# A new order for the instructions of all five engines in a two-layer linear-attention and SwiGLU kernel

## The chip, the cores and the metric

The kernel runs on one core of a Trainium2 chip. The metric is the device time in microseconds (us) of one execution. Five engines work side by side: TensorE (PE in the profile; its weight loads PEld), VectorE (DVE), ScalarE (ACT), GpSimd (POOL) and SyncE (SP), which here only issues DMA transfers.

## What is computed

Two layers on x of 2048 rows and 512 columns, each a linear attention with 32 heads and a gated MLP with 1792 hidden columns, both behind a layer norm and added to x:

```
def _A_ref(x, wqkv, wo):
    qkv = (x @ wqkv).reshape(B, S, 3, H, Dh) ...
    phi = lambda t: jnp.where(t > 0, t + 1, jnp.exp(t)) + 1e-6
    pq, pk = phi(q), phi(k)
    kv = jnp.einsum("bhsd,bhse->bhde", pk, v)
    z = jnp.einsum("bhsd->bhd", pk)
    o = einsum("bhqd,bhde->bhqe", pq, kv) / (einsum("bhqd,bhd->bhq", pq, z)[..., None] + 1e-6)
    return o ... @ wo

def _B_ref(x, w1, w3, w2):
    return (_silu(x @ w1) * (x @ w3)) @ w2

x = x + _A_ref(_layernorm(x), wqkv, wo)
x = x + _B_ref(_layernorm(x), w1, w3, w2)
# and both once more, with the same weights
```

## The kernel before

Each product is made of three matmuls of 16-bit parts: every operand is split into a high and a low part (fp16), and high by high, high by low and low by high are added in PSUM (`mm`, L947). The products of the MLPs and of the second attention are further cut into 2 x 2 blocks, of which seven products instead of eight are made (`products7`).

The work runs in stages. First the keys of layer 0, 16 tiles of 128 rows (`keys_turn`): ScalarE and another engine make high and low parts of a tile, SP issues a DMA transpose (L1858), `keep_transposed` stores an earlier tile's transpose to DRAM (L1875) for use by the queries, and PE makes the keys (`pk`) and the Gram products (`gt`). Then the queries, the MLP of layer 0, and from about 545 us on the second attention (`attention7`). Its keys go in 8 pairs of tiles (`pair_turn`): ScalarE (L1586) and POOL (L1587, L1588, L1589) split the pair's rows, SP issues a transpose of 12 blocks (L1590); ScalarE (L1591) and POOL (L1592) split the sums of rows that the seven products need, and SP issues a transpose of 16 blocks (L1593) and a store of the pair (L1594). PE makes the seven products into the banks kb, ka and kc; ScalarE takes a bank (L1634) or VectorE adds it (L1638), which frees it for the next product. The feature map follows (L1675 to L1681), and PE's Gram products `gt`. The layer norm's scale is POOL's: L917 to L921, with a pow in L918, and ScalarE's L924 applies it.

The queries (about 640 to 735 us) read the pair's transposes back from DRAM (`load7`, L1685), make seven products into qb, qa and qc, and the exp of L1717 and L1718. Then come the weighing (L1732 to L1753), the split (L1759 on ScalarE, L1760 on POOL), a transpose (L1769) and the output product `po`, which VectorE and ScalarE add to x (L1953 to L1958). The MLP of layer 1 starts on the first of these rows, and its last sums are stored to the output (L2127).

What sets the order on every engine is a table: `ORDER` (L72 to L475) holds for each engine a permutation of the instructions in the sequence in which the code issues them, and `arrange` makes each instruction depend on the one ahead of it in the table, with no wait between engines:

```
for engine, text in ORDER.items():
    at = []
    for part in text.split():
        first, _, last_ = part.partition("-")
        at.extend(range(int(first), int(last_ or first) + 1))
    for before, after in zip(at, at[1:]):
        tc.add_manual_dep(traced[engine][after], traced[engine][before].name, ...NoSync...)
```

An engine runs its list in that order and stops at the first instruction whose inputs or buffers are not ready, whatever stands behind it. SP's list is the order in which the transfers are issued.

Of the kernel before, what the change touches and what calls it, by code (L numbers as in the profile page):

```python
# [73 lines left out]
        "0-20 22-23 26-27 24 28 25 30 29 34 38-39 35-36 21 31-32 37 40-41 33 42-65 78-89 66-77 "  # L74
        "102-113 90-92 96-101 93-95 126-137 120-122 114-116 123-125 117-119 150-161 144-149 "
        "162-173 138-140 174-176 183-185 141-143 180-182 177-179 186-197 201-203 198-200 204-209 "
        "228-230 225-227 210-224 231-245 258-269 255-257 249-254 246-248 276-278 282-293 279-281 "
        "306 300-302 307 303-305 308-319 270-272 326-328 273-275 294-299 323-325 350-352 347-349 "
        "329-331 353-355 332-343 320-322 377-379 344-346 356-367 380-391 404 371-373 405-406 "
        "374-376 398-400 368-370 401-403 395-397 392-394 416-418 407-409 413-415 419-421 410-412 "  # L80
        "425-427 431 422-424 428-430 432-455 460-471 456-458 472-483 459 484-555 568-579 556-567 "
        "592-603 616-627 580-591 604-615 628-651 664-675 652-663 688-699 676-687 712-723 700-711 "
        "736-747 760-771 724-735 748-759 772-808 821-832 809-820 833-868 893-904 869-880 905-910 "
        "917-928 881-892 911-916 941-958 965-970 929-934 1001-1006 935-940 971-976 959-964 "
        "1007-1012 977-988 1109 1013-1018 1049-1054 1110-1111 1085-1090 1019-1024 1112 1117-1120 "
        "1055-1060 989-994 1121 1113 1122 1114 995-1000 1115-1116 1373-1374 1125 1381 1126 1375 "
# [82 lines left out]
        "3780-3781 3784-3785 3815-3816 3788-3789 3722-3727 3786-3787 3728-3733 3764-3769 "  # L169
        "3752-3757 3819-3820 3734-3745 3821-3822 3831 3823-3828 3857-3862 3791-3796 3803-3808 "  # L170
        "3817-3818 3833 3797-3802 3809-3814 3829 3835 3832 3848-3849 3834 3830 3836-3837 "
        "3863-3868 3838-3839 3844-3847 3840-3841 3856 3850 3842-3843 3854 3852 3855 3853 3851 "
        "3869-3874 3917-3918 3893-3898 3875-3880 3921-3924 3899-3904 3881-3886 3905-3910 "
        "3887-3892 3911-3916 3925-3926 3962-3967 3933 3919-3920 3931 3927-3928 3935 3929-3930 "
        "3968-3973 3998-4002 3937 3934 3950-3961 4034-4035 3938-3943 4042 4026-4029 4003 "
        "3944-3949 3932 3974-3979 4038-4039 4022-4023 3936 4024-4025 3980-3985 4030-4031 "
        "4067-4070 4036-4037 4081 4032-4033 4004-4009 3986-3991 4010-4015 4040-4041 4082 "
        "4088-4089 3992-3997 4071-4076 4083 4079-4080 4016-4021 4077-4078 4109-4114 4090-4091 "
        "4087 4084 4145-4150 4102 4092-4093 4115-4120 4055-4060 4151-4156 4061-4066 4094-4095 "
        "4100-4101 4121-4126 4085 4108 4104-4105 4157-4162 4103 4127-4132 4043-4048 4086 "  # L180
        "4169-4170 4163-4168 4133-4138 4096-4097 4139-4144 4049-4054 4098-4099 4106 4214-4219 "
        "4173-4174 4220-4225 4250-4255 4171-4172 4107 4190-4195 4202-4213 4175-4176 4185 4183 "
        "4177-4178 4181-4182 4189 4184 4274-4275 4286-4287 4226-4231 4196-4201 4179-4180 "
        "4256-4261 4232-4237 4276-4277 4262-4267 4186 4278-4279 4288 4280-4281 4187 4290 4294 "
        "4289 4291 4188 4238-4249 4268-4273 4319-4320 4282-4285 4323-4324 4321-4322 4292 "
        "4333-4334 4340-4341 4293 4325-4326 4307-4312 4327-4328 4335-4336 4313-4318 4295-4300 "
        "4331-4332 4342-4343 4354 4301-4306 4382-4387 4329-4330 4355 4388-4393 4412-4417 "
        "4337-4338 4348-4349 4339 4352-4353 4350-4351 4344-4345 4358 4360 4359 4394-4405 "
        "4346-4347 4356-4357 4406-4411 4361-4362 4365-4366 4487-4492 4363-4364 4481-4486 "
        "4367-4368 4375 4369-4370 4377 4373-4374 4376 4371-4372 4418-4421 4432-4433 4381 "  # L190
        "4379-4380 4426-4427 4430-4431 4438 4378 4428-4429 4422-4425 4434 4436 4435 4439-4440 "
        "4437 4499-4504 4493-4498 4441-4446 4517-4522 4455-4456 4464-4465 4447-4448 4511-4516 "
        "4453 4466-4467 4454 4476 4449-4450 4460-4461 4457-4458 4468-4469 4477 4470-4471 "
        "4462-4463 4478-4479 4451-4452 4474 4459 4472-4473 4480 4475 4535-4540 4505-4510 "
        "4523-4525 4553-4558 4526-4534 4544-4549 4541-4543 4565-4570 4559-4564 4550-4552 "
        "4577-4588 4601-4606 4571-4576 4595-4597 4592-4594 4610-4612 4598-4600 4589-4591 "
        "4613-4615 4607-4609 4619-4624 4616-4618 4631-4636 4625-4630 4649-4654 4643-4648 "
        "4661-4663 4637-4642 4667-4672 4664-4666 4655-4657 4679-4681 4658-4660 4685-4690 "
        "4682-4684 4673-4678 4697-4702 4691-4696 4715-4720 4709-4714 4703-4708 4733-4738 "
        "4724-4729 4742-4744 4730-4732 4721-4723 4745-4747 4751-4756 4739-4741 4748-4750 "  # L200
        "4763-4768 4757-4762 4781-4786 4775-4780 4769-4774 4799-4804 4790-4798 4787-4789 "
        "4814-4816 4811-4813 4805-4810 4817-4828 4847-4852 4859-4861 4829-4834 4856 4835-4846 "
        "4862-4864 4877-4879 4865-4870 4857-4858 4880-4882 4874-4876 4883-4888 4853-4855 "
        "4871-4873 4895-4900 4889-4894 4913-4918 4907-4912 4973-4978 4901-4906 4931-4936 "
        "4928-4930 4922-4924 4979-4990 5003-5008 4946-4948 4919-4921 4991-4996 4940-4942 "
        "4937-4939 4997-5002 4949-4951 4961-4963 5009-5014 4925-4927 5015 4952-4954 5016-5021 "
        "4964-4966 4943-4945 5028-5033 4958-4960 5110-5115 5040-5045 5022-5027 4955-4957 "
        "4967-4972 5052-5057 5122-5127 5034-5039 5116-5121 5046-5051 5058-5069 5134-5139 "
        "5070-5106 5128-5133 5107-5109 5146-5151 5140-5145 5152-5169 5206-5212 5170-5181 "
        "5213-5217 5182-5199 5230-5241 5200-5205 5218-5229 5260-5265 5296-5301 5242-5247 "  # L210
        "5272-5283 5254-5259 5284-5295 5266-5271 5248-5253 5302-5307 5326-5331 5308-5313 "
# [2246 lines left out]
```

## Time and profile before

| | |
|---|---|
| median of 3 runs | 1137.07 us (1136.81 to 1137.78) |
| span of the profiled execution | 1134.0 us |
| PE busy | 1123.7 us, 99% |
| DVE busy | 849.3 us, 75% |
| ACT busy | 663.2 us, 58% |
| POOL busy | 429.7 us, 38% |

The profile is one execution. PE's matmuls are pipelined, and the stated end of one lies behind the start of the next; a stall is therefore read as the distance of two starts less the spacing of the matmuls between them. The idle time in brackets behind a row is what the profile counts between the stated end and the next start, with the engine or transfer that ended it.

### The profile page before, as it was taken

The page shows a single profiled execution, that of the slowest core. Times are in us where ns is not written, and L with a number is a line of the kernel's source. Part 1 is how long each engine was busy: PE and PEld are TensorE (multiplying, and loading weights), DVE is VectorE, ACT ScalarE, POOL GpSimd, SP SyncE. Part 2 cuts the span into 40 slices and gives each one's busy share as a digit, 9 for nine tenths or more (in the row PEclk, how much of TensorE's full clock was granted, in tenths as well). Part 3 has the DMA queues.
Part 4 walks back from the last instruction along what each step waited for, and adds up shares of the span by engine and source line. Part 5 has one row for each costly group of instructions (what it writes and reads, how often), then busy time and mean ns, then how long its engine had stood idle before and what let it go on. Part 6 is the DMA issues. An engine that isn't in the chain of part 4 may idle for free.

```text
span 1134.0 us, 22473 instructions
## 1 busy us (share of the span) xinstructions
PE 1123.7 (99%) x9117; PEld 888.3 (78%) x9117; DVE 849.3 (75%) x1468; ACT 663.2 (58%) x1104; POOL 429.7 (38%) x477
## 2 busy tenths in 40 slices
PE   8999999999999999999999999999999999999998
PEld 3445446888888888888886676578888888888887
DVE  7789878896978887889896488847855666465556
ACT  7668878775544445455578666686544434343442
POOL 6731796502001222335678416862152110302113
PEclk9999999999999999999999999999999999999999
DMA  8995665389673332331267946643482440220001
GB/s 258 304 292 181 174 136 121 75 220 272 204 279 122 117 149 103 112 155 66 48 179 177 276 165 153 114 89 105 120 240 102 177 178 1 85 84 29 11 20 57
DMA packets 171768, 162.94 MB, mean 144 GB/s; under 512 B 139536, under 2 KB 147984, under 8 KB 167056
## 3 DMA queue, kind: packets, MB, share of 16 engines
q1 hardware_dynamic: 171664, 161.51, 48.7%
q8 instruction: 71, 1.16, 0.4%
q14 instruction: 33, 0.27, 0.1%
HBM read 80.08 MB, written 47.32 MB: 112 GB/s over the span
## 4 chain that ended last, share of the span: by engine, by line
PE 91%; DVE 2%; POOL 2%; DMA 2%; issue 1%; ACT 1%; SPq 0%; DVEq 0%; POOLq 0%; ACTq 0%
PE bb L947 26%; PE po L2097 20%; PE bc L947 13%; PE ba L947 6%; PE gt L947 6%; PE po L947 5%; PE pq L947 4%; PE pk L947 3%; PE po L2117 3%; DMA arena<-arena 2%; PE kb L947 1%; PE qb L947 1%; PE kc L947 1%; PE kv L947 0%; PE qc L947 0%
## 5 line engine op out<-in xcount | busy, mean ns | idle before, releaser
L947 PEld LDWEIGHTS <-arena 128*128 128x128 f16 x6648 | 646.1, 98 | 204.5 <-DMA arena<-arena 4.4
L947 PE MATMUL bb<-arena 128*128 128x256 f16 x2688 | 349.2, 273 | 0.0
L2097 PE MATMUL po<-arena 128*128 128x256 f16 x2058 | 288.5, 273 | 0.0
L2052 ACT ACTIVATE arena<-bb 128x512 f32<-128x512 f32 x196 | 115.3, 594 | 195.5 <-PE bb L947 166.7
L2097 PEld LDWEIGHTS <-arena 128*128 128x128 f16 x2058 | 201.3, 98 | 23.4
L947 PE MATMUL bc<-arena 128*128 128x256 f16 x1344 | 179.6, 273 | 0.0
L2055 DVE TENSOR_TENSOR arena<-arena,bc 128x512 f32<-128x512 f32 x112 | 76.7, 685 | 87.5 <-PE bc L947 54.1
L2007 ACT ACTIVATE arena<-arena,scalars 128x512 f32<-128x512 f32 x112 | 74.6, 666 | 90.2 <-DVE arena L2055 70.2
L2146 DVE SCALAR_TENSOR_TENSOR arena<-po,scalars,arena 128x256 f32<-128x256 f32 (+1 forms) x180 | 101.5, 585 | 31.7 <-PE po L2097 21.7
L2013 DVE TENSOR_TENSOR arena<-arena 128x1280 f16<-128x1280 f32 (+1 forms) x90 | 105.4, 1174 | 21.2 <-ACT arena L2011 20.8
L2011 ACT ACTIVATE arena<-arena 128x512 f16<-128x512 f32 (+1 forms) x112 | 101.0, 904 | 32.2 <-DVE arena L2026 13.7
L2008 DVE SCALAR_TENSOR_TENSOR arena<-arena,scalars 128x512 f32<-128x512 f32 x112 | 78.6, 705 | 34.5 <-ACT arena L2007 34.4
L947 PE MATMUL ba<-arena 128*128 128x256 f16 x672 | 91.8, 273 | 0.0
L947 PE MATMUL gt<-arena 128*128 128x512 f16 x384 | 89.6, 379 | 0.0
L947 PE MATMUL po<-arena 128*128 128x512 f16 x384 | 86.8, 379 | 0.5 <-DMA arena<-arena 0.5
L2013 POOL TENSOR_TENSOR arena<-arena 128x512 f16<-128x512 f32 x22 | 27.0, 1228 | 115.0 <-ACT arena L2011 108.2
L2155 POOL TENSOR_TENSOR arena<-arena 128x512 f32<-128x512 f32 x27 | 38.0, 1406 | 81.7 <-DVE arena L2146 81.7
L2154 POOL TENSOR_TENSOR arena<-arena 128x512 f32<-128x512 f32 x27 | 37.1, 1375 | 71.4 <-DVE arena L2146 69.3
L871 DVE SCALAR_TENSOR_TENSOR arena<-arena,scalars 128x512 f16<-128x512 f32 (+2 forms) x74 | 59.1, 814 | 2.3 <-ACT arena L869 2.2
L924 ACT ACTIVATE arena<-arena,nb_all,rs_all 128x512 f32<-128x512 f32 x64 | 50.8, 806 | 13.2 <-POOL nb_all L921 7.6
L2023 POOL TENSOR_TENSOR arena<-arena 128x256 f32<-128x256 f32 x10 | 7.9, 786 | 131.3 <-DVE arena L2008 131.3
L869 ACT ACTIVATE arena<-arena,scalars 128x512 f16<-128x512 f32 (+2 forms) x74 | 52.2, 718 | 5.2 <-DVE arena L1003 2.3
(234 smaller groups left out, 1449.4 us busy)
## 6 DMA issues: line engine op xcount, KB each, us to landing
arena<-xb_d SPq DMA_DIRECT2D x12, 1792.0 KB, 8.0
xb_d<-arena SPq DMA_DIRECT2D x8, 1792.0 KB, 7.7
w_d<-arena SPq DMA_DIRECT2D x5, 1792.0 KB, 7.6
arena<-w_d SPq DMA_DIRECT2D x5, 1792.0 KB, 8.0
arena<-in_B_w_dram SPq DMA_DIRECT2D x8, 896.0 KB, 7.0
arena<-in_B_w_dram SPq DMA_DIRECT2D x28, 256.0 KB, 3.0
xt_d<-arena SPq DMA_DIRECT2D x8, 896.0 KB, 5.1
arena<-xt_d SPq DMA_DIRECT2D x8, 896.0 KB, 6.7
```

What stands on the lines that cost most here:

```text
L869: nc.scalar.activation(hi, src, AF.Copy, scale=scale)
L871: lambda: nc.vector.scalar_tensor_tensor(lo, src, scale, hi, OP.mult, OP.subtract)
L924: nc.scalar.activation(dst, x_sb[:, t, :], AF.Identity, scale=rs_all[:, t : t + 1], bias=nb_all[:, t : t + 1],)
L947: nc.tensor.matmul(dst, lhs(a, k), rhs(b, k), start=first and k == 0 and i == 0, stop=last and k == n - 1 and i == len(PASSES) - 1, skip_g ...
L2007: nc.scalar.activation(t, gate, AF.Silu, scale=info["u1"])
L2008: nc.vector.scalar_tensor_tensor(t, up, info["hid"], t, OP.mult, OP.mult)
L2011: nc.scalar.activation(hs[:, 0, lo:hi], t[:, lo:hi], AF.Copy)
L2013: engine.tensor_tensor(hs[:, 1, lo:hi], t[:, lo:hi], hs[:, 0, lo:hi], OP.subtract)
L2052: nc.scalar.activation(dst, bank_, AF.Copy)
L2055: nc.vector.tensor_tensor(dst, dst, bank_, OP.add)
L2097: nc.tensor.matmul(po[:, i * HALF : (i + 1) * HALF], hs[:, a, qx, cs], w2[:, b, qw, :], start=g == ends[0] and i + a + b == 0, stop=g == e ...
L2146: nc.vector.scalar_tensor_tensor(dst, src, cb, to, OP.mult, OP.add)
```

## The change

Only the table `ORDER` is new. Each engine's list is another permutation of the same instructions: on PE 864 of 9100 stand at another place, on VectorE 439 of 1436, on ScalarE 272 of 1051, on POOL 176 of 475, on SP 120 of 307, by at most 25 places and on average by about one. The table is 8 lines longer, so the same line of code has a number that is higher by 8 in the changed kernel. The lists differ from before in the first keys (20 to 195 us), from about 500 to 735 us, in single places up to 935 us, and in the last 40 us. There are four loads of ScalarE's function tables in both. Two lines of the diff show its kind:

```diff
-        "102-113 90-92 96-101 93-95 126-137 120-122 114-116 123-125 117-119 150-161 144-149 "
...
+        "66-77 102-113 90-92 99-101 93-98 126-137 117-119 123-125 114-116 150-161 120-122 "
```

On SP, at the tiles 2 to 4 of the first keys, before (L962 loads a weight, L2319 a tile of x, L1875 stores a tile's transpose, L1858 is the transpose):

```order
L1875 DMA xt_d<-arena 128x1024
L1858 DMA_TRANSPOSE arena<-arena 128x8x128
L962 DMA arena<-in_B_w_dram 128x1792
L1875 DMA xt_d<-arena 128x1024
L1858 DMA_TRANSPOSE arena<-arena 128x8x128
L2319 DMA arena<-in_A_x_dram 128x512 x2
L1875 DMA xt_d<-arena 128x1024
```

and after:

```order
L1883 DMA xt_d<-arena 128x1024
L2327 DMA arena<-in_A_x_dram 128x512 x2
L1866 DMA_TRANSPOSE arena<-arena 128x8x128
L970 DMA arena<-in_B_w_dram 128x1792
L1883 DMA xt_d<-arena 128x1024 x2
L1866 DMA_TRANSPOSE arena<-arena 128x8x128
```

Two loads of x have moved ahead of tile 3's transpose (the first one here), and the store of tile 3, which stood behind tile 4's transpose, stands ahead of it, beside the store of tile 2.

On SP again, in the keys of the second attention from pair 3 to pair 5, before (L1590 and L1593 are a pair's transposes, L1594 its store):

```order
L1590 DMA_TRANSPOSE arena<-arena 128x12x128
L1593 DMA_TRANSPOSE arena<-arena 128x16x128
L1590 DMA_TRANSPOSE arena<-arena 128x12x128
L1593 DMA_TRANSPOSE arena<-arena 128x16x128
L1594 DMA xt_d<-arena 128x3584 x2
L1590 DMA_TRANSPOSE arena<-arena 128x12x128
L1593 DMA_TRANSPOSE arena<-arena 128x16x128
L1594 DMA xt_d<-arena 128x3584
```

and after:

```order
L1598 DMA_TRANSPOSE arena<-arena 128x12x128
L1601 DMA_TRANSPOSE arena<-arena 128x16x128
L1602 DMA xt_d<-arena 128x3584
L1598 DMA_TRANSPOSE arena<-arena 128x12x128
L1601 DMA_TRANSPOSE arena<-arena 128x16x128
L1602 DMA xt_d<-arena 128x3584
L1598 DMA_TRANSPOSE arena<-arena 128x12x128
L1601 DMA_TRANSPOSE arena<-arena 128x16x128
```

The store of pair 3 has moved from behind the transposes of pair 4 to the place ahead of them.

On POOL, between the L1592 of pair 5 and that of pair 6, before:

```order
L1592 TENSOR_TENSOR arena<-arena 128x1024
L1654 COPY arena<-scalars 128x2
L917 TENSOR_SCALAR ve<-mv_all 128x2
L920 TENSOR_SCALAR neg<-mv_all 128x2
L1588 TENSOR_TENSOR arena<-arena 128x512
L918 TENSOR_TENSOR rs_all<-ve,minus_half 128x2
L1587 CAST arena<-arena 128x2x256
L1589 TENSOR_TENSOR arena<-arena 128x2x256
L921 TENSOR_TENSOR nb_all<-neg,rs_all 128x2
L1592 TENSOR_TENSOR arena<-arena 128x1024
```

and after:

```order
L1600 TENSOR_TENSOR arena<-arena 128x1024
L1662 COPY arena<-scalars 128x2
L928 TENSOR_SCALAR neg<-mv_all 128x2
L925 TENSOR_SCALAR ve<-mv_all 128x2
L926 TENSOR_TENSOR rs_all<-ve,minus_half 128x2
L929 TENSOR_TENSOR nb_all<-neg,rs_all 128x2
L1596 TENSOR_TENSOR arena<-arena 128x512
L1595 CAST arena<-arena 128x2x256
L1597 TENSOR_TENSOR arena<-arena 128x2x256
L1600 TENSOR_TENSOR arena<-arena 128x1024
```

The pow and the product behind it (L918 and L921 before) have moved ahead of the pair's first subtraction.

Four more moves are named below. On SP the load of L1685 (a pair's transposes for the queries, 896 KB) has moved from behind the store of pair 2, at 589.87 us in the profile before, to the place ahead of pair 2's transposes, behind pair 0's store. On PE a Gram product has moved ahead of the kb product at 616.14, and the products of qa and qb change places around 717 us. On ScalarE a take of a kb bank (L1634) has moved ahead of L1680 at about 621 us, and an L924 ahead of the exp of L1717 at about 718 us.

## Rows read from the trace of the kernel before

**Rows 1.** The page: span, busy time by engine, PE's granted clock in 40 slices.

```profile
span 1134.0 us, 22473 instructions
...
PE 1123.7 (99%) x9117; PEld 888.3 (78%) x9117; DVE 849.3 (75%) x1468; ACT 663.2 (58%) x1104; POOL 429.7 (38%) x477
...
PEclk9999999999999999999999999999999999999999
```

**Rows 2.** Timeline of PE, 26 to 32 us: start, duration, engine, line, operands, count.

```profile
26.23 2.75 PE L947 MATMUL gt<-arena 128*128 128x512 f16 x12
29.29 2.76 PE L947 MATMUL pk<-arena 128*128 128x512 f16 x12 [0.30 <-DMA arena<-arena]
```

**Rows 3.** Timeline of SP's issues, 22 to 26 us: start, time to issue.

```profile
22.75 1.26 SPq L1858 DMA_TRANSPOSE arena<-arena  x1
24.07 1.47 SPq L2319 DMA_DIRECT2D arena<-in_A_x_dram  x2
```

**Rows 4.** Chain of waits, 20 to 34 us, then DMA issues at 24.07 (last: to landing).

```profile
22.75 6.49 DMA arena<-arena
...
arena<-in_A_x_dram SPq DMA_DIRECT2D x1, 256.0 KB, 5.8
```

**Rows 5.** Timeline of PE, 609 to 635 us.

```profile
609.75 2.11 PE L947 MATMUL gt<-arena 128*128 128x512 f16 x9
612.70 0.83 PE L947 MATMUL kb<-arena 128*128 128x256 f16 x6 [0.84 <-DMA arena<-arena]
...
615.33 0.82 PE L947 MATMUL kc<-arena 128*128 128x256 f16 x6
616.14 0.82 PE L947 MATMUL kb<-arena 128*128 128x256 f16 x6
...
632.03 0.82 PE L947 MATMUL kb<-arena 128*128 128x256 f16 x6
633.46 0.83 PE L947 MATMUL kc<-arena 128*128 128x256 f16 x6 [0.61 <-DMA arena<-arena]
```

**Rows 6.** Timeline of SP's issues, 606 to 610 us.

```profile
606.70 1.92 SPq L1593 DMA_TRANSPOSE arena<-arena  x1
608.72 4.32 SPq L1594 DMA_DIRECT2D xt_d<-arena  x2
```

**Rows 7.** DMA issues: the L1593 transposes of 597.4, 606.7, 618.0 (us to landing).

```profile
arena<-arena SPq DMA_TRANSPOSE x1, 4.3
...
arena<-arena SPq DMA_TRANSPOSE x1, 6.0
...
arena<-arena SPq DMA_TRANSPOSE x1, 4.2
```

**Rows 8.** Timeline of POOL, 620 to 625 us.

```profile
620.99 1.45 POOL L1588 TENSOR_TENSOR arena<-arena 128x512 f16<-128x512 f32 x1 [2.08 <-ACT arena L1586]
622.40 1.76 POOL L918 TENSOR_TENSOR rs_all<-ve,minus_half 128x2 f32<-128x2 f32 x1
```

**Rows 9.** Timeline of PE, 694 to 734 us.

```profile
699.12 0.82 PE L947 MATMUL qa<-arena 128*128 128x256 f16 x6
699.78 1.47 PE L947 MATMUL qb<-arena 128*128 128x256 f16 x12
701.54 0.81 PE L947 MATMUL qc<-arena 128*128 128x256 f16 x6 [0.29 <-ACT arena L1634]
...
722.66 10.52 PE L947 MATMUL po<-arena 128*128 128x512 f16 x48
733.70 0.60 PE L947 MATMUL po<-arena 128*128 128x512 f16 x2 [0.52 <-DMA arena<-arena]
```

**Rows 10.** Timeline of ACT, 719 to 720 us.

```profile
719.13 0.81 ACT L924 ACTIVATE arena<-arena,nb_all,rs_all 128x512 f32<-128x512 f32 x1
```

**Rows 11.** SP's issue at 584.22, its landing, and PE's first use of it.

```profile
584.22 3.46 SPq L1593 DMA_TRANSPOSE arena<-arena  x1
...
arena<-arena SPq DMA_TRANSPOSE x1, 5.2
...
591.20 0.82 PE L947 MATMUL kb<-arena 128*128 128x256 f16 x6
```

444 rows, old and new, of the table ORDER are left out of this document.

## Prediction

> **What bounds the kernel now.** I read the page first: the span is 1134.0 us, TensorE (PE) is busy for 1123.7 us of it, and its granted clock stands at the upper of the two levels (2.4 GHz) in every slice [rows 1]. So nothing can be gained but the moments in which PE stands still; a shorter list on another engine is worth nothing by itself. The view to find those moments is PE's timeline. Its stated busy times end later than the next start, so I go from start to start. The even spacing comes from two groups of the same matmul: 48 take 10.52 us and 12 take 2.75 [rows 2, 9], so (10.52 - 2.75) / 36 = 0.216 us for one of 512 columns; of 256 columns 12 take 1.47 and 6 take 0.82 [rows 9], so 0.65 / 6 = 0.108 us. Whatever lies between two starts beyond that is a stall.
>
> Done for the whole program this gives about 11 us of stall, of which 5.5 lie in the first 14 us, ahead of everything that the change touches, and about 0.8 in short steps that it leaves alone. What remains after the first scores is some 4.6 us, in few places: 0.47 at 29.29 (12 matmuls from 26.23 should end at 28.82) [rows 2]; 1.00 at 612.70 (9 from 609.75 end at 611.70) and 0.77 at 633.46 (6 from 632.03) [rows 5]; 0.45 at 701.54 (12 from 699.78) and 0.68 at 733.70 (48 from 722.66 take 10.36 and not 11.04), [rows 9]; the rest, read in the same way, are one of 0.20 and some of 0.15 or less, such as the one at 616.14 (0.81 where 0.65 is due) [rows 5]. The whole prize is therefore 4.6 / 1134 = 0.4%. The three runs' median is 1137.07, the profiled execution's span 1134.0, so 3.07 us lie around the span; I add that to whatever span I work out. A difference of 0.2% (2.3 us) is about the least that measuring this kernel can tell from none.
>
> **The change part by part.** Each engine keeps its instructions, tiles and durations; only their order is new, so each term is a wait that appears or goes.
>
> *The first keys.* On SP's queue two loads of x tiles (L2319) now stand ahead of the transpose of tile 3, and the store of tile 3's transposed keys (L1875) stands ahead of the transpose of tile 4 (L1858). That transpose was issued at 22.75 [rows 3] and landed 6.49 us later, at 29.24 [rows 4], which is what PE waited for at 29.29. The store has to wait on SP for tile 3's transpose to land and is one issue more, so tile 4's issue comes about a us later, and it has one more 256 KB transfer in front of it. The x load issued behind it at 24.07 [rows 3] landed 5.8 us after, at 29.87 [rows 4], 0.63 after the transpose: that is the passage of one such transfer. I take 0.63 plus some 0.2 for the two x loads that are now in front of tile 3 (most of their passage falls in time that the queue had free): +0.8. The ends: 0, if the queue is not what holds the transpose back; +1.7, if the two x loads also pass in full (0.63 x 2 = 1.26, less a share that the later stall takes over).
>
> *Keys of the second attention, 590 to 633.* Three edits meet here. First, SP: the store of pair 3's transposed tile (L1594) stood behind the transposes of pair 4, and was issued at 608.72, two us after the transpose that PE waited for (606.70) [rows 6]. That transpose took 6.0 us to land, while those of the same size issued at 597.4 and 618.0, with nothing right behind them, took 4.3 and 4.2 [rows 7]. Now the store goes out as soon as pair 3's own transpose has landed (597.40 + 4.3 = about 601.7) and is gone when pair 4's second transpose is issued. With 4.3 it lands at 606.70 + 4.3 = 611.0, ahead of the 611.70 at which PE wants it: -1.00. What the store then stands in front of is pair 4's first transpose, which had about 1 us of slack. Second, POOL: L918's pow (1.76 us, at 622.40) and L921 move from between L1588 and L1589 into the 2.08 us in which POOL was idle ahead of L1588 at 620.99 [rows 8]. Everything behind it in pair 6 (L1587, L1589, L1592, then the transpose of 16 blocks) comes some 1.7 us earlier, and PE's wait at 633.46 was 0.77: gone. DVE's statistics, which the pow needs, are done by then. Third, PE puts Gram products in front of the kb product at 616.14, and ScalarE takes a kb bank ahead of L1680: 0.15 and 0.15. Sum -2.07. Ends: a transpose with a store right ahead of it took 5.2 [rows 11]; by that pair 4's lands at 611.9 and 0.2 of the 1.00 stays; and if the store's move brings nothing, -1.07 is left.
>
> The rows show that a transfer issued two us behind goes with 1.7 us more to landing [rows 6, 7]. The Trainium skill, DMA: Bandwidth & Descriptors, section Queues, rings and completion order, states that on each DMA engine descriptors are consumed in ring order; by that a store behind a transpose can't hold it back, and the 1.00 would stay (a rival, below). The three landings of this trace speak against it.
>
> *Between 574 and 591.* The 896 KB load of L1685 stood behind all of pair 2's transfers and now stands ahead of its two transposes. The second of these was issued at 584.22 and took 5.2 us to land [rows 11], that is at 589.4; PE's first matmul on it started at 591.20, without a stall, so 1.8 us were to spare. How long 896 KB hold the queue I bound from the 256 KB above: 3.5 x 0.63 = 2.2 us if everything passes at that pace, and up to 1.5 times that, 3.3, beside other traffic. The load can start some 1 us before the first of the transposes is issued, and with the 1.8 to spare that covers 2.8 us. I take 0; the end is 3.3 - 2.8 = 0.5 for the load, and another 1.0 if the store between the two transposes is pushed back into the second, +1.5.
>
> *Queries, 690 to 735.* The stall at 701.54 and a small one of 0.10 before it stay in sum, since the same two ScalarE takes now wait for each other in another order. The one of 0.20, at 722.01, and one of 0.09 go, as PE's products of qa and qb change places: -0.29. Against that, ScalarE now runs the layer norm's L924 (0.81 us [rows 10]) ahead of the exp of L1717, on which L1718, then the chain L1732 to L1753, L1759, L1760 and the transposes of L1769 hang, that is the 0.68 at 733.70. It eats free time on ScalarE first; I put 0.25 on the chain, and 0.25 on a qb take that now stands behind a wait. Together +0.2, ends -0.8 and +0.8.
>
> *Everything else.* Swaps between 500 and 574 and from 735 to 935 stand where there was no stall, though in many places with only 0.05 to 0.5 us of slack. At the end the last add and the last store wait for PE's last matmul as before; only the order of the ones ahead changes. Both 0, the first with +1 at its far end.
>
> The sum is 0.8 - 2.07 + 0 + 0.2 = -1.07 us: a span of 1132.9 and a time of 1136.0 us. All best ends give 1134.2, all worst 1140.
>
> **The rivals.** *All waits in reach go.* If the first transposes are not held by the queue (0 instead of +0.8) and the query chain profits too (0.10 + 0.45 + 0.29 + 0.68 = 1.52 instead of +0.2 the other way), the sum is -2.07 - 1.52 = -3.6: 1133.5. For it: each of these waits ends on one engine's order, and orders are just what changes. Against: the transfers of the start land one right behind the other [rows 4], and ScalarE's moves go the wrong way for the 0.68.
>
> *The store's move brings nothing.* If the slow transpose of 606.70 had another cause than the store behind it, the 1.00 stays and the sum is -0.07: 1137.0. Against it speak the three landings [rows 7]; there are only three. (By the ring order that the Trainium skill states, in the section named above, this is the case to expect.)
>
> *The transfers moved ahead cost more than they free.* This is the slower one. SP's queue gets four transfers in front of transposes that PE needs soon: two x loads and a store at the start, the 896 KB load at 580; and pair 3's store stands before pair 4's first transpose, too. If each passes in full ahead of the transpose, the start costs 1.7, 580 costs 1.5, and the keys keep only -0.9, with +0.2 from the queries: +2.5, 1139.6 us. It decides from the point where the load holds the queue for over 2.8 us, and where tile 3's transpose lands after 23.6. For it: that the queue was full at 22 to 30. Against: at 580 there is slack.
>
> **How the numbers follow.** The forecast as worked out 0.46, the store without effect 0.15, all waits go 0.27, transfers cost more 0.12. The first two lie within 0.2%, so same 0.61, faster 0.27, slower 0.12. The likeliest is 1136.0. For the range I go down past 1133.5 (to 1133.2), since the second case is common enough, and up to 1139.2, just short of the slower case's middle: about 0.1 is left out at each side.
>
> **What would show it.** In the profile after: PE's start with tile 4's keys should come some 0.8 us later against the matmuls ahead of it, the stall of the kb group that stood at 612.70 and of the kc group at 633.46 should be gone, the L1593 transpose of pair 4 should land in about 4.3 us, and the po group that stood at 733.70 should wait as long as before or longer. A stall of more than half a us anywhere between 500 and 592 would prove the 0 there wrong; a granted clock below the upper level anywhere would spoil all of it.

## The result: slower by 0.2%, and the profile after

| | before | after |
|---|---|---|
| median (15 runs each) | 1137.07 us (1136.39 to 1139.70) | 1138.92 us (1136.65 to 1144.45) |
| ratio to before, 95% interval | | 1.0019 (1.0010 to 1.0028) |
| span of the profiled execution | 1134.0 us | 1136.3 us |

The forecast was 1136.0 us, 1.1 less than before. The kernel became 1.85 us slower in the median (1.1 to 3.2 by the interval), and its times spread over 8 us instead of 3. Executions that took over 1.5% longer than the fastest of the same kernel (two of e6 and one of e10, below) are in no median, ratio or spread here.

The page of the kernel after: PE is as busy as before, and its granted clock reads as before [rows 1].

```profile
PE 1124.9 (99%) x9117; PEld 888.6 (78%) x9117; DVE 850.8 (75%) x1468; ACT 662.5 (58%) x1104; POOL 430.8 (38%) x477
...
PEclk9999999999999999999999999999999999999999
```

The difference of the two spans, 2.3 us, has to be found in stalls. I read it as how much later PE starts its n-th matmul than in the trace before, at the borders of the stages:

| stage (us of before) | forecast | profile after | e13 | e14 |
|---|---|---|---|---|
| 10 to 18, where nothing was changed | 0 | +1.3 | +1.1 | +1.0 |
| 18 to 205, first keys | +0.8 | +1.9 | +3.1 | +4.7 |
| 205 to 645, second keys | -2.1 | -0.4 | -0.1 | 0.0 |
| 645 to 735, queries | +0.2 | -0.7 | -0.5 | -0.6 |
| 735 to the end | 0 | 0.0 | -0.1 | -0.1 |

(e13 and e14 are two more executions of the changed kernel, below.) The first row is not the change. PE's windows of the kernel after and then of before (length, busy time and count by engine, PE's granted clock, DMA share and GB/s) show a clock at the lower level, 1.2 GHz, from 12 us to about 15 us in the one and not in the other:

```profile
12.00:14.00 2.00, 2.00 (x10) 0.93 (x8) 1.86 (x5) 1.97 (x4) 1.83 (x3) 0.50 0.70 265
14.00:16.00 2.00, 2.00 (x8) 0.79 (x7) 1.97 (x7) 1.73 (x4) 0.25 (x2) 0.67 1.06 261
```

```profile
12.00:14.00 2.00, 1.82 (x12) 0.85 (x10) 1.88 (x5) 1.97 (x5) 1.83 (x3) 1.00 0.65 246
14.00:16.00 2.00, 2.00 (x11) 0.86 (x9) 1.97 (x10) 1.63 (x4) 0.22 (x2) 1.00 1.26 284
```

PE had stood still for 2.57 us just before in the one case and for 2.23 us in the other, waiting for POOL. Of the 17 traces other than e11's, those of before and after among them, 12 have the lower clock, whatever the order, and it cost them 1.0 to 1.3 us; the profile before was one of the five without it. The length of the standstill does not tell the two cases apart: in e5 it was 1.95 us and the clock fell, in e6 it was 2.40 and it did not.

In the rest, the timeline of PE after shows at 30.21, without idle time, the start that waited at 29.29 before [rows 2]; PE came to that place 1.39 us later (27.62 after 26.23), most of it from the lower clock. New stalls stand at other places:

```profile
27.62 2.75 PE L955 MATMUL gt<-arena 128*128 128x512 f16 x12
30.21 1.03 PE L955 MATMUL pk<-arena 128*128 128x512 f16 x4
...
46.42 1.89 PE L955 MATMUL gt<-arena 128*128 128x512 f16 x8
49.29 2.32 PE L955 MATMUL gt<-arena 128*128 128x512 f16 x10 [0.98 <-DVE arena L1413]
...
180.17 2.75 PE L955 MATMUL po<-arena 128*128 128x512 f16 x12
183.29 1.90 PE L955 MATMUL po<-arena 128*128 128x512 f16 x8 [0.38 <-DMA arena<-arena]
...
591.70 2.97 PE L955 MATMUL gt<-arena 128*128 128x512 f16 x13
595.84 0.83 PE L955 MATMUL kb<-arena 128*128 128x256 f16 x6 [1.18 <-DMA arena<-arena]
```

From start to start these are 1.14 us at 49.29 (8 matmuls need 1.73 and took 2.87), 0.53 at 183.29 and 1.33 at 595.84. The chain of waits of the kernel after leads from 49.29 back to a load of x:

```profile
42.87 4.79 DMA arena<-in_A_x_dram
...
47.69 0.71 DVE st L917
...
48.60 0.65 DVE arena L1413
...
49.29 0.81 PE gt L955 x3
```

VectorE stands in its new order at the layer-norm statistics (L917) of a tile of x whose load the new order of SP issued at 42.87. What PE needs, L1413 (L1405 before: the low part of the keys), had its input at about 45.5 us and stood behind the statistics on the same engine. In the kernel before the load was issued at 40.25 and landed at 43.5.

The chain that ends at 595.84 goes through the second transpose of pair 2, ahead of whose two transposes the change moved the load of 896 KB:

```profile
585.48 2.29 POOL arena L1600
...
587.82 7.97 DMA arena<-arena
...
595.84 0.83 PE kb L955 x6
```

Before, the same transpose took 5.2 us to land [rows 11]; now 7.97. Of the other two places of the second keys one went as forecast and one by half: at 616.31 the kb group follows without a stall, and at 636.39 the kc group waits 0.41 (from 635.33: 1.06 where 0.65 is due) instead of 0.77 [rows 5]:

```profile
614.37 2.11 PE L955 MATMUL gt<-arena 128*128 128x512 f16 x9
616.31 0.82 PE L955 MATMUL kb<-arena 128*128 128x256 f16 x6
...
635.33 0.82 PE L955 MATMUL kb<-arena 128*128 128x256 f16 x6
636.39 0.83 PE L955 MATMUL kc<-arena 128*128 128x256 f16 x6 [0.24 <-DMA arena<-arena]
...
724.91 10.52 PE L955 MATMUL po<-arena 128*128 128x512 f16 x48
735.99 1.25 PE L955 MATMUL po<-arena 128*128 128x512 f16 x5 [0.55 <-DMA arena<-arena]
```

In the queries the wait of 0.45 at 701.54 [rows 9] is gone, and the last, at 735.99, is 0.71 after 0.68.

### The profile page after: what moved, and what is told of

It is laid out like the page before. It is cut to its first block, busy times and chain, and to the rows that moved or that the text cites. A ratio compares the mean times of both kernels' runs of the same rounds, so it can differ in the third digit from the quotient of the medians.

```text
span 1136.3 us, 22475 instructions
## 1 busy us (share of the span) xinstructions
PE 1124.9 (99%) x9117; PEld 888.6 (78%) x9117; DVE 850.8 (75%) x1468; ACT 662.5 (58%) x1104; POOL 430.8 (38%) x477
## 3 DMA queue, kind: packets, MB, share of 16 engines
q8 instruction: 71, 1.16, 0.4%
## 4 chain that ended last, share of the span: by engine, by line
PE 91%; POOL 3%; DMA 3%; DVE 1%; issue 1%; ACT 1%; SPq 0%; POOLq 0%; DVEq 0%
PE bb L955 26%; PE po L2105 19%; PE bc L955 13%; PE ba L955 6%; PE gt L955 6%; PE po L955 5%; PE pk L955 3%; PE po L2125 3%; PE pq L955 3%; DMA arena<-arena 2%; PE qb L955 2%; PE kb L955 1%; DMA arena<-in_A_x_dram 1%; PE qc L955 1%; PE kc L955 1%
## 5 line engine op out<-in xcount | busy, mean ns | idle before, releaser
L2021 DVE TENSOR_TENSOR arena<-arena 128x512 f16<-128x512 f32 (+1 forms) x90 | 105.7, 1178 | 21.7 <-ACT arena L2019 21.4
```

The costliest lines, as they stand in the source:

```text
L2021: engine.tensor_tensor(hs[:, 1, lo:hi], t[:, lo:hi], hs[:, 0, lo:hi], OP.subtract)
```

## The experiments

Most of these kernels take one part of the new table and leave the rest old; e4, e11 and e12 move a single entry of the old one. The ratio is to executions of the kernel before on the same chip, beside them; the stages are read from one trace each, as in the table above.

| run | median us | before | ratio, 95% interval | 18 to 205 | 205 to 645 | 645 to 735 |
|---|---|---|---|---|---|---|
| e1 start only | 1140.18 | 1136.56 | 1.0033 (1.0020 to 1.0046) | +3.7 | +0.3 | 0.0 |
| e2 late only | 1137.79 | 1136.56 | 1.0011 (1.0001 to 1.0021) | -0.5 | -0.4 | -0.7 |
| e3 late, load back | 1137.21 | 1136.56 | 1.0003 (0.9994 to 1.0012) | -0.5 | -1.4 | -0.1 |
| e4 load ahead | 1137.83 | 1136.56 | 1.0010 (1.0001 to 1.0019) | -0.5 | +1.5 | 0.0 |
| e5 second keys, load back | 1135.54 | 1136.86 | 0.9989 (0.9980 to 0.9998) | -0.5 | -1.5 | +0.1 |
| e6 queries and rest | 1137.19 | 1136.86 | 1.0003 (0.9994 to 1.0012) | +1.5 | +0.2 | +1.5 |
| e9 queries, POOL later | 1138.65 | 1137.10 | 1.0013 (1.0004 to 1.0022) | +0.2 | +0.5 | +1.2 |
| e10 start, x first | 1140.07 | 1137.10 | 1.0025 (1.0016 to 1.0035) | +1.1 | +0.5 | +0.6 |
| e12 store ahead | 1136.60 | 1136.96 | 0.9999 (0.9990 to 1.0008) | +0.5 | -0.8 | 0.0 |
| e15 start, SP only | 1138.33 | 1136.62 | 1.0017 (1.0008 to 1.0026) | 0.0 | -1.0 | 0.0 |
| e16 start, all but SP | 1142.98 | 1136.62 | 1.0058 (1.0046 to 1.0071) | +5.3 | +0.1 | +0.6 |

An execution of an unchanged part differs from the trace before by up to 0.6 us (the old start stands at -0.5 to +0.5, once at +1.5 with a wait of 0.85 at 188 us that no other trace has, and e15's old keys at -1.0 because the 1.00 of [rows 5] is absent there). The trace alone therefore settles nothing under a us; a wait that stands in one kernel's every trace and in none of the other's does.

### Which part: start or late

```diff
 ORDER, every engine:
-    old up to 300 us, old behind
+    new up to 300 us, old behind
```

> The new order up to 300 us alone (the first keys and all behind them up to the first layer's MLP), the old one from there. Theory A, the start is what costs: the profile of the changed kernel has stalls of 1.15 us (Gram products waiting for DVE's L1413, which stands behind bn_stats of a late tile of x), 0.20, 0.23 and 0.54 before 200 us that the kernel before has not, and lacks its 0.46: +1.5 to +2.0 us against the kernel before, about 1139. Theory B, the start costs nothing and the loss lies behind 500 us: no difference, 1137, and those stalls don't come back. Theory C, the loss is a lower granted clock at 12 to 16 us that comes by chance: no difference in the mean of many executions, and the stalls above cost nothing more than they show.

```diff
-    old up to 300 us, old behind
+    old up to 300 us, new behind
```

> The old order up to 300 us, the new one from there. Theory A: the new stall of 1.34 us at pair 2's kb product and the waits that went (1.00, 0.37 of 0.77, 0.45, 0.29, three of 0.15) come out at about -1.1 us, some 1136. Theory B: +1.9, 1139. Theory C: about -1.1 as well.

The start alone costs 3.6 us in the median, more than all of the change. PE's timeline of e1 has the stall of 1.14 again, at 47.79, and a second one of 1.66 ahead of 60.69, for a transpose of the keys that landed 7.6 us after its issue, behind two weight loads of 896 KB:

```profile
44.93 1.89 PE L953 MATMUL gt<-arena 128*128 128x512 f16 x8
47.79 2.32 PE L953 MATMUL gt<-arena 128*128 128x512 f16 x10 [0.97 <-DVE arena L1411]
...
58.38 0.81 PE L953 MATMUL gt<-arena 128*128 128x512 f16 x3
60.69 1.69 PE L953 MATMUL pk<-arena 128*128 128x512 f16 x7 [1.50 <-DMA arena<-arena]
```

Theory A holds for the start, with more than it said (3.6 against 1.5 to 2.0); C (the clock alone) falls. The late part lost its stalls in the trace as expected (-1.2 behind 205 us), but not in the median: 1.2 slower. The trace is of the quickest of its 11 executions (1135.47), and these spread over 4.7 us. That was the second question. The two losses add to 4.8 us, where the whole change lost 1.85.

### The load of 896 KB

```diff
 L1594 DMA xt_d<-arena
+L1685 DMA arena<-xt_d
 L1590 DMA_TRANSPOSE arena<-arena
 L1594 DMA xt_d<-arena
 L1593 DMA_TRANSPOSE arena<-arena
 L1594 DMA xt_d<-arena
-L1685 DMA arena<-xt_d
```

> The kernel before with one entry of SP's list moved: the load of L1685 ahead of pair 2's two transposes, as in the changed kernel. Theory L: the transpose issued at about 584 lands some 2.8 us later than before, past the 1.8 us to spare, a stall of about 1 us at pair 2's kb product, 1138. The rival (POOL's order): no stall there, 1137.

The reverse on top of e2, the load back at its old place:

> As e2_late_only, but on SP the 896 KB load of L1685 stands again behind pair 2's store, where it stood before. Theory L, the load ahead of the two transposes is what made the second of them land in 8.0 us instead of 5.2: the stall of 1.34 is gone and this is 1.3 us faster than e2_late_only, -2.4 against the kernel before, 1134.7. The rival, that the transpose was late for another reason (POOL issues it later in the new order): the stall stays and nothing is gained over e2_late_only.

e4 is the kernel before with this one entry moved, and its chain of waits reads as that of the changed kernel:

```profile
586.02 7.94 DMA arena<-arena
...
594.01 0.83 PE kb L953 x6
```

A stall of 1.27 us, and +1.3 us in the median. In e3 the stall is gone, though its median, 1137.21, is only 0.6 under that of e2 and not the 1134.7 expected: the spread again. Theory L is shown: one transfer ahead on SP goes with a stall of 1.2 to 1.5 us in each of five traces that have it (after, e2, e4, e13, e14) and with none in those that don't.

The DMA packets of that landing show that the load makes only half of it. Before, the transpose's last data packet ended 4.56 us after the issue and the landing came 0.6 later; in the profile after the data ended 5.97 us after the issue, 1.4 later, and the landing came 2.0 behind that. In that second gap, in all five traces, a packet of PE's instructions runs on one of the DMA engines (more on it below, at the store of pair 3). With the 0.6 of before the transpose would have landed at about 594.4 (587.82 + 5.97 + 0.6), when PE wanted it at 594.5 (13 matmuls from 591.70): by this estimate the load alone would have used up the slack and cost about nothing.

### Where the spread comes from

```diff
+    new from 300 to 640 us, but L1685 at its old place; old elsewhere
```

> The new order from 300 to 640 us alone (the end of the first MLP and the second attention's keys), with the load of L1685 at its old place; the old order ahead and behind. The profile of e3_late_load_back has 1.4 us less stall up to 642 us than the kernel before, though its times spread over 4.5 us (1134.5 to 1139.0) where those of the kernel before spread over 2.5. If the spread comes from the keys: median about the kernel before, spread of 4 us again. If it comes from the queries and what is behind: a median 1.4 us under the kernel before, 1135.2, with its narrow spread.

```diff
+    new from 640 us on; old ahead
```

> The new order from 640 us to the end alone (queries, second MLP, the tail). By the profile of e3_late_load_back -0.2 us against the kernel before: 1136.4 with a narrow spread, if the spread of e3 comes from the keys; about +1.5 in the median and a spread of 4 us if it comes from here.

And the kernel of e3 twice more:

> The kernel of e3_late_load_back once more, for another trace. If its times spread because a wait turns up in some executions and not in others, the list of PE's stalls differs from that of e3's profile at one or two places, by 1 to 3 us in sum; if the spread lies ahead of 16 us (granted clock, first loads), the lists behind 300 us agree within 0.3 us.

> The same kernel a third time, with the same two expectations as e7.

e5 is 1.3 us faster than the kernel before, with a spread of 2.4 us: the only kernel here whose interval lies under 1 (1135.54 against 1136.86; it ends at 0.9998). e6 has the spread, 1135.0 to 1139.6, but not the +1.5 in the median (+0.3). The traces of e6, e7 and e8 (1139.62, 1137.07 and 1136.56 us) have three stalls that e2, e3 and the changed kernel lack, 0.92, 0.36 and 0.97 us, and e7 and e8 are the same kernel as e3 (1134.48); in e6:

```profile
708.04 0.82 PE L953 MATMUL qc<-arena 128*128 128x256 f16 x6
709.61 0.81 PE L953 MATMUL qa<-arena 128*128 128x256 f16 x6 [0.75 <-DVE arena L1644]
...
720.38 0.82 PE L953 MATMUL qa<-arena 128*128 128x256 f16 x6
721.99 0.81 PE L953 MATMUL qb<-arena 128*128 128x256 f16 x6 [0.80 <-ACT arena L1640]
```

The cause stands in the timelines of VectorE and POOL. In e3 (its L1756 is L1749 of the kernel before, a small operation on the denominators):

```profile
705.00 0.19 DVE L1756 TENSOR_SCALAR arena<-arena 128x64 f32<-128x64 f32 x1
...
705.01 1.20 POOL L2001 TENSOR_TENSOR arena<-arena 128x512 f16<-128x512 f32 x1
```

and in e6 (L1755 and L2000 there):

```profile
707.97 1.20 DVE L1755 TENSOR_SCALAR arena<-arena 128x64 f32<-128x64 f32 x1
709.08 0.47 DVE L1644 SCALAR_TENSOR_TENSOR arena<-qc,scalars,arena 128x256 f32<-128x256 f32 x1
...
707.95 1.16 POOL L2000 TENSOR_TENSOR arena<-arena 128x512 f16<-128x512 f32 x1
```

The same two operations start within 0.02 us of each other. Where VectorE is 0.01 ahead it takes 0.19 us; where POOL is 0.02 ahead, VectorE's operation takes 1.20 and ends when POOL's does (707.95 + 1.16 = 709.11). The take behind it (L1644 at 709.08) comes a us late, which is PE's wait at 709.61, and further on its L1738, which takes 1.35 us in e3, takes 2.92 beside another POOL operation. In the kernel before, the same operation of VectorE started at 705.11 and the next one of POOL at 705.25: 0.14 us of distance. The new order brought the two to a tie. The exclusion itself is in the old order too, at other places: at 693.55 of the kernel before the same operation took 0.92 us and ended with POOL's L1760.

By the Trainium skill, SBUF — State Buffer, section Who interferes with whom, an operation of VectorE in a two-port mode and one of GpSimd exclude each other for the whole instruction, and the one that starts first decides who waits. The traces agree: 0.19 against 1.20 us. That L1749 runs in such a mode is not shown by any of them.

To test it, POOL's three next steps were put behind its L1760 in e6's order, so that POOL is idle beside L1749:

```diff
 L1981 TENSOR_TENSOR arena<-arena 128x256
-L1994 TENSOR_TENSOR arena<-arena 128x512
-L1982 TENSOR_TENSOR arena<-arena 128x256
-L1984 TENSOR_TENSOR arena<-arena 128x256
 L1760 TENSOR_TENSOR arena<-arena 128x2x512
+L1994 TENSOR_TENSOR arena<-arena 128x512
+L1982 TENSOR_TENSOR arena<-arena 128x256
+L1984 TENSOR_TENSOR arena<-arena 128x256
```

> e6_queries_rest with one change on POOL: the three layer-norm steps (L1994, L1982, L1984 in this kernel's order) that start at the same hundredth of a us as DVE's L1749 at about 705 us stand behind the L1760 after them, so POOL is idle there. Theory P, the lock: in e6, e7 and e8 POOL's step started 0.01 to 0.02 us ahead of L1749, which then took 1.20 us instead of 0.19, and PE waited 0.92, 0.36 and 0.97 us at qa, qb and qb. Then L1749 takes 0.2 us here in every execution, these three waits go, and the median is about that of the kernel before, -0.2 us (1136.4), with a spread of 2 to 3 us instead of 4. The rival, that DVE's list alone makes the waits (L1638's add of a qc bank stands behind L1749): they stay, 1138.

VectorE's operation took 0.19 us, the stalls of 0.92 and 0.36 were gone, and the spread shrank to 2.3 us. The median did not fall, since the moved steps are late for ScalarE's L1988 (L1994 here), ahead of the take that frees qb:

```profile
706.30 0.19 DVE L1755 TENSOR_SCALAR arena<-arena 128x64 f32<-128x64 f32 x1
...
715.89 1.06 ACT L1994 ACTIVATE arena<-arena 128x1024 f16<-128x1024 f32 x1 [2.04 <-POOL arena L1990]
...
717.54 0.81 PE L953 MATMUL qa<-arena 128*128 128x256 f16 x6
719.97 0.81 PE L953 MATMUL qb<-arena 128*128 128x256 f16 x6 [1.61 <-ACT arena L1640]
```

That the lock makes the first two stalls is shown. The third, of 0.97 at qb, grew to 1.78 for the late steps of POOL, so the median missed the 1136.4 expected by 2.2 us, and e9 says nothing of what the queries would gain. The changed kernel itself, twice more:

> The changed kernel once more, for a second trace. Theory P (who of DVE and POOL starts first at L1749 by some hundredths of a us): either the three stalls of 0.92, 0.36 and 0.97 us at 708 to 721 us stand in the list, or none of them. The stalls of 1.15 us at 48 and of 1.3 us at pair 2's kb product stand there in both cases. If theory P is wrong, one or two of the three appear alone.

> The changed kernel a third time, with the same expectations as e13.

Both (1139.63 and 1141.33 us) had VectorE ahead by 0.01 us and none of the three stalls. So the lock is not what the changed kernel lost in these executions; whether it is in others of its 15 runs is not shown. What differs between its three traces is the start: +1.9, +3.1 and +4.7.

### What in the start

e1 with one move on SP, the load of x ahead of the weights:

```diff
 L1875 DMA xt_d<-arena
+L2319 DMA arena<-in_A_x_dram
 L2326 DMA arena<-in_A_wqkv_dram
 ...
-L2319 DMA arena<-in_A_x_dram
```

> e1_start_only with one change on SP: the load of a tile of x that DVE's bn_stats wait for at 46 us stands ahead of the weight loads that the new order put in front of it. Theory Q, the queue: the tile lands some 5 us earlier, the stall of 1.14 us goes, and the median is 1.1 us under e1's, 1139.0. The rival, that DVE's order makes the stall whatever the load does: it stays, 1140.2.

```diff
-    old on every engine up to 300 us
+    new on SP up to 300 us, old on PE, DVE, ACT and POOL
```

> The kernel before with SP's new order up to 300 us alone; PE, DVE, ACT and POOL keep the old one. Theory Q, the queue of transfers: SP's order (weight and x loads moved against the transposes) makes most of the 1.9 to 4.7 us that the start of the new order costs between 18 and 205 us in four traces: here 1.5 to 4 us there, median about 1139.5. The rival, the compute engines' order (bn_stats ahead of L1405 on DVE and the like): about 0, 1137.

```diff
-    old on every engine up to 300 us
+    old on SP up to 300 us, new on PE, DVE, ACT and POOL
```

> The converse: the new order up to 300 us on PE, DVE, ACT and POOL, SP's old one. Theory Q: the x tile lands by 43.5 us as before, no stall at 46 to 48 us, 0 to 1 us between 18 and 205 us, median about 1137.3. The rival: the 1.9 to 4.7 us again, 1140. If both e15 and e16 lose, it takes the two orders fitting each other, and neither alone is the cause.

In e10 the stall of 1.14 went and one of 0.75 for POOL's L1372 appeared at 42.96. Its median is 3.0 us over that of the kernel before beside it, where e1's was 3.6; the intervals overlap, so a gain of the 1.1 expected is neither shown nor ruled out. SP's order alone (e15) costs 1.7 us in the median, though its one trace, of its quickest execution, shows nothing between 18 and 205 us. The compute engines' order with SP's old one is the worst of all, 6.4 us. With that theory Q falls: the loss does not need SP's new order. PE's timeline of e16 waits for ScalarE, VectorE and POOL in turn:

```profile
34.04 0.59 PE L953 MATMUL gt<-arena 128*128 128x512 f16 x2 [1.28 <-ACT arena L1402]
35.13 1.67 PE L953 MATMUL gt<-arena 128*128 128x512 f16 x7 [0.50 <-DVE arena L1411]
...
46.32 1.47 PE L953 MATMUL gt<-arena 128*128 128x512 f16 x6 [1.75 <-POOL arena L1372]
```

and VectorE's own timeline shows at what it stood, again the statistics of a tile of x that had not landed:

```profile
30.29 0.69 DVE L915 BATCH_NORM_STATS2 st<-arena 128x6 f32<-128x512 f32 x1 [4.53 <-DMA arena<-in_A_x_dram]
```

As read from this, the new order of the compute engines takes up later tiles earlier, ahead of the steps that PE's next products need, and works only as far as SP brings those tiles in time; the new order of SP does that in part (6.4 us becomes 3.6). Each half loses by itself, and neither alone is the cause. PE's stalls between 18 and 205 us show both in the traces that have the whole new start (after, e13, e14, e1): 1.1 to 2.0 us for VectorE's L1413 behind the statistics, and 0.7 to 2.4 for transposes, where the kernel before has 0.46. Which of the some hundred moves of VectorE, ScalarE and POOL is the first that should be taken back was not tried.

### The store of pair 3

```diff
 L1593 DMA_TRANSPOSE arena<-arena
+L1594 DMA xt_d<-arena
 L1590 DMA_TRANSPOSE arena<-arena
 L1593 DMA_TRANSPOSE arena<-arena
-L1594 DMA xt_d<-arena
 L1594 DMA xt_d<-arena
```

> The kernel before with one entry of SP's list moved: the store of pair 3's transposed tile ahead of pair 4's two transposes. By the prediction the transpose of 606.7 lands in 4.3 us instead of 6.0, and the stall of 1.00 us goes. The rival (a transfer behind a transpose can't hold it back): it lands in 5 to 6 us, the stall stays, or moves to pair 4's first transpose, which then has the store in front of it.

> The kernel of e11 once more, since TensorE's granted clock was low all through that execution, which moves everything on PE against the transfers. In e11 the transpose in question landed in 6.0 us though nothing stood behind it. In the traces a 16 KB packet of instructions (queue q8) runs for 0.95 us on one of the DMA engines inside each of the landings of 5.2 to 6.0 us, and in none of those of 4.2 to 4.3. Theory F, the fetch: the packet comes when PE is at a certain matmul, at about 610.7 us at the full clock; the transpose lands in 4.5 us if its last data packet is done by then and in 6.0 if not, whatever stands behind it; with the store out of the way its data end at about 610.6, so it may fall either way. The prediction's theory: it lands in 4.3 and the 1.00 us goes in every execution: median 1.0 us under the kernel before, 1136.1.

In e11 PE's granted clock was 0.851 on average (1299.72 us), so its time is not compared; a transpose's landing can be, and it was 6.0 us with no transfer behind. The DMA view of that landing (queue, kind, packets, MB, share) has a line that the view of the 4.3 us of the kernel before [rows 7] has not, that of q8:

```profile
q8 instruction: 1, 0.02, 1.0%
...
arena<-arena SPq DMA_TRANSPOSE x1, 6.0
```

A packet of 16 KB of instructions (q8) runs on one of the DMA engines for 0.95 us. These packets are PE's, by their places: 71 of them stand in a trace of 9117 matmuls, one for 128, and this one starts while PE is at its 4698th or 4699th matmul in each of the 17 traces other than e11's. In the kernel before that is 610.66, 4.0 us after the transpose was issued. In e12, at the full clock, it starts 0.09 us after the transpose's last data, the transpose lands in 4.6 us, and the stall of 1.00 is gone; the median is 0.4 us lower, which its interval does not tell from none, where 1.0 was expected.

The store behind is neither needed for the late landing nor enough for it. In e11 it landed in 6.0 without the store. In e15 the store stands 2.0 us behind the same transpose, which landed in 4.7 (issues of SP, then the landing):

```profile
608.61 1.92 SPq L1599 DMA_TRANSPOSE arena<-arena  x1
610.63 3.02 SPq L1600 DMA_DIRECT2D xt_d<-arena  x2
...
arena<-arena SPq DMA_TRANSPOSE x1, 4.7
```

And in the kernel before a later transpose of the same size has a store 2.1 us behind, no packet of instructions, and 4.3:

```profile
637.79 2.04 SPq L1593 DMA_TRANSPOSE arena<-arena  x1
639.92 0.86 SPq L1594 DMA_DIRECT2D xt_d<-arena  x1
...
arena<-arena SPq DMA_TRANSPOSE x1, 4.3
```

What tells the landings of 6.0 apart is the gap behind the data. In all 18 traces the data of pair 4's transpose end 3.9 to 4.1 us after the issue, with or without the store. In 10 of them it lands 0.6 us after that, in 8 it lands 2.0 after. In the kernel before, one of the late ones, the packet of instructions ran from 610.66 to 611.62, and two of the transpose's closing writes of 4 bytes came only at 611.61 and 611.62, at its end; in e15 they came at 612.62 and 612.63, and the packet right behind them, at 612.64. It is so without exception: in the 8 late landings, and in the five of pair 2's transpose behind the load, two closing writes come at the end of the packet, and in the 10 others the packet starts behind all of them. Who goes first, by some hundredths of a us in most of them, decides over 1.4 us. The store's place goes with the outcome in 16 of the 18 traces (late in 7 of 8 with it behind, in 1 of 10 without); how it tips that order is not shown.

## Why the prediction was wrong, step by step

- **What bounds the kernel** was right: nothing but stalls of PE moved, and the clock stayed at its upper level behind 16 us.
- **The time around the span** was wrong. I took 3.07 us from one execution's span and other executions' median. Every execution lists 1.7 us outside its span (1137.98 with 1136.3 for the profile after), so the profiled execution of before was a quick one, some 1.4 us under its median. It was one without the low clock at 12 to 16 us. It shifted both kernels alike.
- **The first keys, +0.8 (0 to +1.7)**: this is the step that failed first of all. I costed SP's two moves as a longer wait for tile 4's transpose, and read VectorE's, ScalarE's and POOL's moves there not at all. That wait did not grow: 0.44 in e1, whose clock did not fall, after 0.47 before, and 0 to 0.4 in the three traces of the changed kernel, where the lower clock had made PE late. The stage costs 1.9 to 4.7 us in four traces (after, e13, e14, e1) by waits that the sum did not have: 1.1 to 2.0 with VectorE standing at the statistics of a tile that has not landed and PE's product queued behind it, and the rest for the most part by later transposes. Which move makes how much of it stays open.
- **574 to 591, 0 (to +1.5)**: the second step that failed; the far end of the range came true, +1.2 to +1.5. The queue's part was sized about right: the load moved the end of the transpose's data by 1.4 us, just inside the 1.8 to spare. The landing grew by 2.8 (5.2 to 7.97) since a packet of PE's instructions came ahead of the transpose's closing writes, 1.4 us that no term of the sum had. That the end of the range held it is luck: 1.0 of that end was put there for the store between the two transposes.
- **590 to 633, -2.07**: -1.4 and -1.5 in e3 and e5. The 1.00 and two of 0.15 went; of the 0.77 only 0.1 to 0.4 did (0.41 to 0.65 left), since pair 6's transpose was issued 1.6 us earlier as forecast (628.23 to 626.65 in e5), but landed in 5.3 us again. POOL's step was right. The reason given for the 1.00, that the store behind holds the transpose up, was wrong: the landing is late when the packet of instructions goes ahead of its closing writes, with the store (7 traces) and without it (e11), and e15 has the store and 4.7 us. The 1.00 went as forecast, but not by the mechanism forecast; why the store's place goes with the outcome in 16 of 18 traces stays open. The Trainium skill's ring order (DMA: Bandwidth & Descriptors, Queues, rings and completion order), which I set aside on three landings, agrees with e15 and with a fourth landing of the trace I had, that of 637.79 with a store 2.1 us behind and 4.3 us.
- **690 to 735, +0.2**: -0.5 to -0.7 in the changed kernel (the 0.45 went, which I had left standing, the 0.68 stayed, as forecast), but +1.5 to +1.9 in e6, e7 and e8, where POOL is first at L1749. I did not weigh the lock at all. It came out both ways within one order (e3 against e7 and e8).
- **The rivals**: the slower one, that the transfers moved ahead cost more than they free, gave 1139.6 at 0.12, against 1138.92 measured; that is close in part by luck. Its place at 580 was right; its price for the start, 1.7, is what SP's order alone costs in the median of e15, but the whole new start costs 3.6 (e1), and the compute engines' order, which the rival did not have, is part of that. I should have given it more: in many places where the change touched the path there was under 1 us of slack.

## What to carry to other kernels

Where PE is at 99%, a new order of the other engines can win the few waits that are left and lose new ones. Try it by stretches and take only those that hold in the median of many executions (here the second keys without one load, 0.11% faster); leave the old order where the new one puts work for later tiles ahead of what PE needs next. Before a compute step is moved ahead, look at when its input lands, not only at when its engine is free. Two operations of VectorE and GpSimd that start within some hundredths of a us of each other made these queries 1.6 to 2.0 us longer in some executions of one kernel than in others (e7 and e8 against e3); read the spread of the times as well as their median. Before a late landing is put down to the transfer behind it, look for a landing of the same trace that has such a transfer and is not late.

## What the runs showed of the hardware

- A packet of PE's instructions, 16 KB on queue q8, runs for 0.95 us on a DMA engine that the kernel's transfers use, one for 128 matmuls, here every 10 to 28 us. In the kernel before, the L1593 transposes without one landed in 4.2 to 4.3 us (597.40, 617.97, 637.79), those with one amid their data in 5.6 and 5.2 (571.97, 628.23), and the one with it ahead of its closing writes in 6.0 (606.70), 2.0 us after its last data instead of 0.5.
- VectorE's L1749 (128x64) takes 0.19 us when it starts 0.01 us ahead of POOL's operation (e3), and 1.20 when it starts 0.02 us behind it (e6), and then ends when POOL's does.
- PE's granted clock fell to 0.5 for about 3 us from 11 or 12 us on in 12 of 17 traces, behind standstills of PE of 1.95 to 3.16 us; in the other five, without the fall, they were 1.04 to 2.40 us long.
